# Reordering the start of an attention-and-experts kernel, with shared banks, other weight pieces and a scaling moved to ScalarE

## The chip, the cores and the metric

The kernel runs on one core of a Trainium2 chip. The metric is device time in microseconds (us) for one execution. One profiled execution of each kernel gives a trace; its span is about 2 us shorter than the time of the same execution. Engines are named as in the profile: PE is TensorE's matmuls, PEld its weight loads (they overlap PE), DVE is VectorE, ACT is ScalarE, POOL is GpSimd, SP is the engine that issues the transfers. PEclk is the clock granted to TensorE, with 1.00 as full speed.

A ratio is the mean time of one kernel's fast runs over that of the other's of the same rounds on the same chip, so it is not quite the ratio of the medians that stand beside it.

## The reference, cut to what matters

A linear attention with decay over 4 batches, 8 heads, 768 positions and 48 channels gives x of 3072 x 384. Then four experts, each 384 to 1024 to 384 with a relu, are summed with weights made from `domain_probs`.

```python
# attention, per position t
cur = einsum('bhd,bhe->bhde', u * kt, vt)
y[:, :, t] = einsum('bhd,bhde->bhe', rt, state + cur)
state = w * state + einsum('bhd,bhe->bhde', kt, vt)
# experts
p = domain_probs / (domain_probs.sum(-1, keepdims=True) + 1e-09)
for e in range(4):
    h = maximum(x @ w1[e], 0.0)
    out += p[:, e:e + 1] * (h @ w2[e])
```

## The kernel before

Attention goes in 24 chunks of 128 positions; four chunks, one of each batch, make a group. A chunk passes through these steps: RK (R and K scaled by powers of the decay, two products on DVE; the product `ruk` and the rounded `Vb` on POOL beside them), its transposes RKT, the products At, their mask AtM, Y and its sum Ysb, the state S, and the transpose xTe that feeds the experts.

The experts go in slots, one for each expert and group: layer 1 is 8 F blocks of 3 matmuls of 512 columns with a relu each, layer 2 is four times 8 matmuls of 384 columns. Attention steps of later chunks are woven in between. Every layer's product lands in one of four banks of PSUM with the tag "mm". The first group has no earlier work to hide behind, so its four chunks and expert 0 are written out by hand, with filler matmuls (`spin`) that keep the clock up.

Weights arrive as f32 in three pieces an array and are rounded to bf16 by ACT, DVE and POOL, one piece each.

```python
def load_w1(e):                       # 3 pieces, one for each 128 rows of the input dimension
    for db in range(NDB):
        t = staged[1, e, db] = work.tile([128, 3 * Dm], F32, tag="wst", bufs=8, name="wst")
        nc.sync.dma_start(t[:, 0:F], w1_v[e][:, db, :])
# ...
def wu_consts():
    nc.scalar.activation(w_row, w_row, AF.Ln)
    ps = psum.tile([128, 2, NP * C], F32, tag="At", bufs=1, name="wu_ps")
    spin(6)
    nc.tensor.matmul(ps[:, 0, 0:HD], ones, w_row, start=True, stop=True)
    nc.tensor.matmul(ps[:, 1, 0:HD], ones, u_row, start=True, stop=True)
# ...
def pre_a(ci):
    Rt, Kt, Vt = ins.pop(ci)
    RK = RKB[ci % NRK]
    nc.vector.tensor_mul(RK[:, 0, :, 0:D], Rt, W1_sd)
    nc.vector.tensor_mul(RK[:, 1, :, 0:D], Kt, W2_sd)
    # ...
    nc.gpsimd.tensor_mul(ruk, Rt, Kt)
    nc.gpsimd.tensor_mul(ruk, ruk, U_sd)
    nc.gpsimd.tensor_copy(Vb, Vt)
# ...
def l1(e, sc, fb, s0, n):             # one F block: a bank and a relu of its own
    # ... 3 matmuls into ps[:, 0:n, :]
    nc.scalar.activation(hTs[:, fb, s0:s0 + n, :], ps[:, 0:n, :], AF.Relu)
# ... in l2:
if e == 0:
    nc.vector.tensor_scalar(oaccs[ci], ps, scalar1=pe, scalar2=None, op0=ALU.mult)
# ... in the schedule, at (slot, place in the slot):
casts = {(0, 4): w2_on(1) + [lambda: (load_w2(2), load(6))],     # w2_on: pieces on A, V, P
         (0, 9): w1_on(2) + [lambda: (load_w1(3), load(7))],     # w1_on: pieces on P, A, V
         (1, 4): w2_on(2) + [lambda: load_w2(3)],
         (1, 8): w1_on(3), (2, 3): w2_on(3)}
```

## Time and profile before

| | before |
|---|---|
| median of 4 runs | 331.14 us (329.76 to 332.17) |
| profiled span | 329.9 us |
| PE, DVE, ACT, POOL busy | 93%, 56%, 45%, 34% |
| PE idle in the first 100 us | 17.6 us of the 23 us in the whole span |
| from the second group's first layer 1 (88.27) to the end | 241.6 us |

The holes of PE are in the first 90 us; the prediction shows the slices, the stretches and the milestones. What it did not show is what VectorE did in the hole just before the loop's second slot (58.86). This is the timeline of the kernel before: start and duration in us, engine, line, operation, output and input, shapes, count.

```profile
56.27 0.78 DVE L85 CAST w_sb<-wst 128x1024 bf16<-128x1024 f32 x1
...
57.36 0.55 DVE L210 TENSOR_TENSOR RK<-Rt,W_sd 128x384 bf16<-128x384 f32 x1
57.48 1.32 POOL L87 CAST w_sb<-wst 128x1024 bf16<-128x1024 f32 x1
57.82 1.39 DVE L211 TENSOR_TENSOR RK<-Kt,W_sd 128x384 bf16<-128x384 f32 x1
```

VectorE rounds a piece of 1024 columns in 0.78 us. POOL rounds its own from 57.48 to 58.80, and the matmul at 58.86 waits for that. In the same hole VectorE scales RK of chunk 5. The first half begins 0.12 us before POOL's rounding and takes 0.55 us; the second begins while POOL rounds, ends 0.41 us after POOL is done, and takes 1.39 us. PE stands anyway, so RK costs nothing here.

The rows of groups concerned (line, engine, operation, tiles, shapes, count; busy us, mean ns; idle time before and its releaser):

```profile
L344 DVE TENSOR_SCALAR oacc<-out_ps,p_nat 128x384 f32<-128x384 f32 x24 | 14.8, 617 | 23.7 <-PE out_ps L338 23.3
...
L211 DVE TENSOR_TENSOR RK<-Kt,W_sd 128x384 bf16<-128x384 f32 x24 | 20.9, 870 | 0.0
```

### The profile page before, as it was taken

Reading aid. Unit: us, or ns where it says so; the run is one execution under the profiler, and the core shown is the slowest. Engines: PE = TensorE matmul, PEld = TensorE weight load, DVE = VectorE, ACT = ScalarE, POOL = GpSimd, SP = SyncE. Lnnn points to the kernel's source line nnn. Section 1 sums busy time; section 2 is a strip of 40 time slices with the busy share of each in tenths; the row PEclk is TensorE's granted clock in tenths of the full one; section 3 lists DMA queues with packets and bytes.
Section 4 is the critical chain, followed back from the end, with each engine's and each line's share of the span. In section 5 each row is a group of like instructions: output and inputs, shape, how many; then the busy total and the mean of one; then the engine's idle time right before and its main releaser. Section 6 shows DMA issues by size and latency. Waiting matters only on the chain.

```text
span 329.9 us, 5731 instructions
## 1 busy us (share of the span) xinstructions
PE 306.9 (93%) x2251; PEld 174.0 (53%) x2286; DVE 184.6 (56%) x336; ACT 147.3 (45%) x260; POOL 111.3 (34%) x145
## 2 busy tenths in 40 slices
PE   7976776797999999999999999999999999999995
PEld 2444553454555555555555555555555555555552
DVE  3578536687657657657656666665644644222222
ACT  3432464555344454445435544544444543444440
POOL 2655602677424424433532541541703300000000
PEclk9999797999999999999999999999999999999999
DMA  7999999982154033054213144303020000110002
GB/s 209 287 221 363 286 263 230 223 241 50 32 119 119 6 69 73 0 145 97 42 32 72 33 121 88 59 16 74 25 74 0 2 0 2 48 47 2 0 2 96
DMA packets 84431, 31.89 MB, mean 97 GB/s; under 512 B 75674, under 2 KB 82844, under 8 KB 84404
## 3 DMA queue, kind: packets, MB, share of 16 engines
q1 hardware_dynamic: 84390, 31.52, 37.5%
q8 instruction: 18, 0.29, 0.4%
q14 instruction: 9, 0.07, 0.1%
q10 hardware_dynamic: 14, 0.00, 0.0%
HBM read 26.79 MB, written 4.72 MB: 96 GB/s over the span
## 4 chain that ended last, share of the span: by engine, by line
PE 86%; DVE 8%; issue 2%; ACT 2%; POOL 1%; POOLq 0%; ACTq 0%; DVEq 0%
PE out_ps L338 37%; PE hT_ps L325 36%; PE RKT_ps L234 3%; PE At_ps L249 2%; PE spin_ps L161 2%; DVE AtM L255 2%; PE Y_ps L273 1%; DVE RK L211 1%; PE St_ps L294 1%; PE xT_ps L312 1%; PE Y_ps L266 1%; ACT RKT L242 1%; DVE RK L210 1%; DVE Ysb L277 1%; DVE oacc L344 1%
## 5 line engine op out<-in xcount | busy, mean ns | idle before, releaser
L329 ACT ACTIVATE hTs<-hT_ps 128x512 bf16<-128x512 f32 (+2 forms) x220 | 114.6, 544 | 132.6 <-PE hT_ps L325 128.2
L325 PE MATMUL hT_ps<-xTe,w_sb 128*128 128x512 bf16 (+2 forms) x625 | 142.3, 355 | 4.4 <-POOL w_sb L87 1.9
L338 PE MATMUL out_ps<-w_sb,hTs 128*128 128x384 bf16 x768 | 140.0, 326 | 0.0
L338 PEld LDWEIGHTS <-hTs 128*128 128x128 bf16 x768 | 72.5, 98 | 51.7
L325 PEld LDWEIGHTS <-w_sb 128*128 128x128 bf16 x660 | 58.2, 99 | 49.6 <-POOL w_sb L87 2.4
L346 DVE SCALAR_TENSOR_TENSOR oacc<-out_ps,p_nat,oacc 128x384 f32<-128x384 f32 x72 | 44.5, 617 | 61.2 <-PE out_ps L338 59.6
L224 POOL TENSOR_TENSOR dv<-Vt,dcoef 128x384 f32<-128x384 f32 x24 | 19.9, 830 | 70.8 <-DVE dcoef L223 70.8
L255 DVE TENSOR_TENSOR AtM<-At_ps,mask 128x512 bf16<-128x512 f32 x48 | 30.9, 686 | 22.9 <-PE At_ps L249 22.9
L306 POOL TENSOR_TENSOR S<-Tn,wC 64x192 bf16<-64x192 f32 x32 | 16.4, 514 | 80.2 <-DVE Tn L305 79.0
L242 ACT COPY RKT<-RKT_ps 128x1024 bf16<-128x1024 bf16 x20 | 20.2, 1012 | 24.3 <-PE RKT_ps L234 24.3
L344 DVE TENSOR_SCALAR oacc<-out_ps,p_nat 128x384 f32<-128x384 f32 x24 | 14.8, 617 | 23.7 <-PE out_ps L338 23.3
L215 POOL TENSOR_TENSOR ruk<-ruk,U_sd 128x384 f32<-128x384 f32 x24 | 25.0, 1042 | 5.2 <-ACT U_sd L173 3.4
L214 POOL TENSOR_TENSOR ruk<-Rt,Kt 128x384 f32<-128x384 f32 x24 | 25.3, 1053 | 4.0 <-DMA Kt<-in_k_dram 2.9
L210 DVE TENSOR_TENSOR RK<-Rt,W_sd 128x384 bf16<-128x384 f32 x24 | 21.2, 882 | 4.4 <-ACT W_sd L171 4.3
L211 DVE TENSOR_TENSOR RK<-Kt,W_sd 128x384 bf16<-128x384 f32 x24 | 20.9, 870 | 0.0
L277 DVE TENSOR_TENSOR Ysb<-Y_ps,dv 128x384 bf16<-128x384 f32 x24 | 13.3, 556 | 10.0 <-PE Y_ps L273 8.6
L234 PE MATMUL RKT_ps<-ident,RK 128*128 128x128 bf16 x192 | 15.5, 220 | 2.7 <-DVE RK L210 1.5
L216 POOL CAST Vb<-Vt 128x384 bf16<-128x384 f32 x24 | 17.4, 724 | 0.0
L234 PEld LDWEIGHTS <-RK 128*128 128x128 bf16 x192 | 12.6, 99 | 7.1 <-DVE RK L210 2.3
L161 PE MATMUL spin_ps<-mask,ident 128*128 128x512 bf16 x41 | 14.1, 477 | 1.8 <-POOL mask masks.py:66 1.8
L223 DVE TENSOR_REDUCE dcoef<-ruk 128x8 f32<-128x384 f32 x24 | 13.0, 544 | 2.0 <-POOL ruk L215 2.0
L313 DVE COPY xTe<-xT_ps 128x384 bf16<-128x384 bf16 x24 | 8.6, 357 | 9.7 <-PE xT_ps L312 9.6
(53 smaller groups left out, 132.8 us busy)
## 6 DMA issues: line engine op xcount, KB each, us to landing
wst<-in_moe_w_dram SPq DMA_DIRECT2D x12, 512.0 KB, 5.2
Rt<-in_r_dram SPq DMA_DIRECT2D x24, 192.0 KB, 2.9
Kt<-in_k_dram SPq DMA_DIRECT2D x24, 192.0 KB, 3.1
Vt<-in_v_dram SPq DMA_DIRECT2D x24, 192.0 KB, 2.7
wst<-in_moe_w_dram SPq DMA_DIRECT2D x8, 576.0 KB, 5.9
out_dram<-oacc SPq DMA_DIRECT2D x24, 192.0 KB, 1.9
wst<-in_moe_w_dram SPq DMA_DIRECT2D x4, 384.0 KB, 6.5
prow<-in_moe_domain_probs_dram SPq DMA_DIRECT2D x1, 48.0 KB
```

What stands on the lines that cost most here:

```text
L161: nc.tensor.matmul(ps, ident, mask[:, None, :].to_broadcast((128, 4, 128)), start=True, stop=True)
L210: nc.vector.tensor_mul(RK[:, 0, :, 0:D], Rt, W1_sd)
L211: nc.vector.tensor_mul(RK[:, 1, :, 0:D], Kt, W2_sd)
L214: nc.gpsimd.tensor_mul(ruk, Rt, Kt)
L215: nc.gpsimd.tensor_mul(ruk, ruk, U_sd)
L234: nc.tensor.transpose(ps[:, i, q, :], s["RK"][:, i, 2 * q:2 * q + 2, :].rearrange("p a b -> p (a b)"), ident)
L242: nc.scalar.copy(s["RKT"], ps)
L255: nc.vector.tensor_mul(s["AtM"][:, j], ps[:, j], mask[:, None, :].to_broadcast((128, NP, C)))
L325: nc.tensor.matmul(ps[:, 0:n, :].rearrange("p a b -> p (a b)"), w1_sb[:, e, db, fb * 128:(fb + 1) * 128], xTe[:, db, s0:s0 + n, :].rearran ...
L329: nc.scalar.activation(hTs[:, fb, s0:s0 + n, :], ps[:, 0:n, :], AF.Relu)
L338: nc.tensor.matmul(ps, hTs[:, fb, s, :], w2_sb[:, e, fb, :], start=(fb == 0), stop=(fb == NFB - 1))
L346: nc.vector.scalar_tensor_tensor(oaccs[ci], in0=ps, scalar=pe, in1=oaccs[ci], op0=ALU.mult, op1=ALU.add)
```

## The change

Its intent is to take waits out of the first 90 us. It has five parts.

1. Preamble: the products for w and u get banks of their own, and 6 + 8 fillers become 2 + 1. The row of u comes over ACT's queue, and the inputs of chunk 2 are issued before expert 0's w2.
2. The first group's order is written anew for each engine: scaling of RK, POOL's part and the diagonal term are separate steps; RKT goes to ACT from chunk 1 on; expert 1 no longer starts before the loop.
3. In the first group four F blocks share a bank and one relu of 512 columns (`l1q`), 8 relus instead of 32.
4. w1 comes in F pieces (3, 3 and 2 blocks of 128 columns, three rows of 384 or 256 each), is rounded by ACT, DVE, ACT, one piece at a place of the slot; w2 keeps its pieces and is rounded the same way. All of expert 0's are rounded by ACT. POOL rounds none.
5. Expert 0's result is scaled by ACT instead of DVE.

```diff
+    PIECES = ((0, 3), (3, 6), (6, 8))
     def load_w1(e):
-        for db in range(NDB):
-            nc.sync.dma_start(t[:, 0:F], w1_v[e][:, db, :])
+        for i, (a, b) in enumerate(PIECES):
+            nc.sync.dma_start(t[:, 0:(b - a) * Dm].rearrange("p (d f) -> p d f", d=NDB),
+                              w1_v[e][:, :, a * 128:b * 128])
# ...
     def wu_consts():
-        ps = psum.tile([128, 2, NP * C], F32, tag="At", bufs=1, name="wu_ps")
-        spin(6)
+        wp = psum.tile([128, HD], F32, tag="ys", bufs=1, name="wu_ps")
+        up = psum.tile([128, HD], F32, tag="mm", bufs=4, name="wu_ps")
+        spin(2)
# ...
+    def l1q(e, sc, fb0, s):
+        ps = psum.tile([128, 4, 128], F32, tag="mm", bufs=4, name="hT_ps")
+        for i in range(4):
+            for db in range(NDB):
+                nc.tensor.matmul(ps[:, i, :], w1_sb[:, e, db, (fb0 + i) * 128:(fb0 + i + 1) * 128],
+                                 xTe[:, db, s, :], start=(i == 0 and db == 0),
+                                 stop=(i == 3 and db == NDB - 1), skip_group_check=True)
+        nc.scalar.activation(hTs[:, fb0:fb0 + 4, s, :], ps, AF.Relu)
# ... in l2
-            nc.vector.tensor_scalar(oaccs[ci], ps, scalar1=pe, scalar2=None, op0=ALU.mult)
+            nc.scalar.mul(oaccs[ci], ps, pe)
# ... the first group, its part around chunks 2 and 3 (the old order of these steps left out)
+        stY(2)
+        scale_rk(3)
+        ruk_vb(3)
+        spin(2)
+        stX(2)
+        stRK(3)
+        p_consts()
+        l1q(0, 0, 0, 2)
+        l1q(0, 0, 4, 2)
# ... the slots
-        casts = {(0, 4): w2_on(1) + [lambda: (load_w2(2), load(6))],
-                 (0, 9): w1_on(2) + [lambda: (load_w1(3), load(7))],
+        casts = {(0, 1): [lambda: cast_w2(1, 0, "A")], (0, 2): [lambda: cast_w2(1, 1, "V")],
+                 (0, 6): [lambda: cast_w2(1, 2, "A"), lambda: (load_w2(2), load(6))],
+                 (0, 7): [lambda: cast_w1(2, 0, "A")], (0, 8): [lambda: cast_w1(2, 1, "V")],
+                 (0, 10): [lambda: cast_w1(2, 2, "A"), lambda: (load_w1(3), load(7))],
# ... likewise for slots 1 and 2
```

## The prediction

> **What bounds the kernel now.** I read the page from the top: busy shares, the 40 slices, the chain that ended last, then the waits, the stretches and the timeline of the first 100 us. One core, span 329.9 us.
>
> ```profile
> PE   7976776797999999999999999999999999999995
> ...
> PEclk9999797999999999999999999999999999999999
> DMA  7999999982154033054213144303020000110002
> ...
> PE 86%; DVE 8%; issue 2%; ACT 2%; POOL 1%; POOLq 0%; ACTq 0%; DVEq 0%
> ```
>
> Each digit is the busy share of 8.2 us, in tenths. PE is full from the eleventh slice on; only the first ten have holes, and there the clock dips twice and the DMA engines are full for some 70 us. The chain of waits is 86% PE, and its non-PE parts lie early. The stretches put numbers on it (length; PE, PEld, DVE, ACT, POOL busy; clock; DMA share; GB/s):
>
> ```profile
> 0.00:16.00 16.00, 13.92 (x64) 5.93 (x65) 6.90 (x26) 6.05 (x10) 7.07 (x16) 1.00 0.88 243
> 16.00:45.00 29.00, 21.46 (x230) 15.11 (x228) 19.75 (x42) 10.76 (x35) 14.06 (x17) 0.94 1.00 279
> 45.00:60.00 15.00, 10.13 (x93) 6.15 (x94) 8.14 (x14) 7.45 (x20) 4.69 (x5) 0.89 0.97 264
> 60.00:76.00 16.00, 15.07 (x127) 8.49 (x127) 12.20 (x21) 9.77 (x15) 9.88 (x14) 1.00 0.87 206
> 76.00:100.00 24.00, 21.82 (x169) 12.26 (x171) 16.23 (x27) 10.53 (x17) 11.97 (x15) 1.00 0.32 74
> 100.00:330.00 230.00, 224.52 (x1579) 126.04 (x1606) 121.35 (x208) 102.71 (x167) 63.62 (x82) 1.00 0.20 47
> ```
>
> PE is idle 5.5 us in the last 230 us, of which some 3.8 us is the tail (last matmul ends at 326.05, then the last sum and the store). In the first 100 us it is idle 17.6 us, and part of its "busy" time there is filler: 41 spin matmuls, 14.1 us. The gain can only come from before the steady state. The timeline fixes the milestones (start, us, engine, line):
>
> ```profile
> 7.29 3.59 PE L161 MATMUL spin_ps<-mask,ident 128*128 128x512 bf16 x8
> ...
> 8.49 0.56 DVE L211 TENSOR_TENSOR RK<-Kt,W_sd 128x384 bf16<-128x384 f32 x1
> ...
> 10.68 0.72 PE L234 MATMUL RKT_ps<-ident,RK 128*128 128x128 bf16 x8
> ...
> 16.10 1.53 PE L325 MATMUL hT_ps<-xTe,w_sb 128*128 128x128 bf16 x24
> ...
> 46.52 1.46 PE L338 MATMUL out_ps<-w_sb,hTs 128*128 128x384 bf16 x8
> ...
> 58.86 0.82 PE L325 MATMUL hT_ps<-xTe,w_sb 128*128 128x512 bf16 x3 [1.93 <-POOL w_sb L87]
> ...
> 73.32 1.46 PE L325 MATMUL hT_ps<-xTe,w_sb 128*128 128x512 bf16 x6
> ...
> 88.27 1.46 PE L325 MATMUL hT_ps<-xTe,w_sb 128*128 128x512 bf16 x6
> ```
>
> These are: the spins that hold PE until 10.88 although RK was ready at 9.05; the first transposes; the first layer 1 (16.1); the start of the loop of slots (46.5); and the first layer 1 of expert 2 (58.9, held by POOL's rounding of its weights), of expert 3 (73.3) and of the second group of chunks (88.3). From there the program is the same but for which engine scales expert 0, so the prediction is how far left the 88.3 moves.
>
> **What the Trainium skill says.** "TensorE: Matmul & The Clock Gate", section "What's actually happening": PE runs at half rate until it has been busy for a window of about 3.4 us, and again after an idle window. The trace agrees: spins are 0.43 us apart until 10.7 us, 0.21 us apart at 11.2; after the 2.45 us wait for Ysb ending at 32.75 the next 24 layer-1 matmuls take 2.48 instead of 1.53 us. So filler may be removed only where real work takes its place. "ScalarE: Activation LUTs", section "What ACT_TABLE_LOAD costs": an ACTIVATE costs a fixed part plus 0.833 ns per element, and a per-partition pointer operand adds 93 ns. The trace agrees: relu of 128 columns 278 ns, of 512 columns 598 ns; the exponential with a pointer scale on 384 columns 582 ns. "SBUF — State Buffer", section "Who interferes with whom": a VectorE instruction with two SBUF inputs contends with GpSimd reads. The trace agrees: RK from Kt takes 0.55 us with POOL idle, 1.35 us beside a POOL product. "DMA: Bandwidth & Descriptors", section "Why small descriptors are slow (HBM only)", explains why 192-byte input rows are worse than weight rows; the trace shows 370 to 390 GB/s in slices of weights alone and 160 to 210 where inputs mix in.
>
> **Part by part.**
>
> Preamble. Before, six cold spins delay the w product to 4.44; with two it starts once the ones are set (that memset ends at 3.35) and ends near 5.1 (1.64 us long). W has its own bank now, so the exponential no longer waits for the u product: 5.2 instead of 7.40, -2.2 us. RK(0) is then ready at about 6.9, and one spin instead of eight lets the transposes start at 7.0, not 10.68: -3.7 us. The chain transposes, RKT, At, AtM, Y, Ysb, xT, xTe took 5.4 us before and is unchanged, so layer 1 could start at 12.5 to 13. Its weights: DMA moved 2.33 MB by 10 us, load 0 and w1 of expert 0 are 0.59 + 1.57 MB; three roundings on ACT (1.15, 1.15, 0.83, from 9.5) end at 12.6. Part: -3.5 us.
>
> Chunks 1 to 3. Before, 16.1 to 46.5, 30.4 us, and with 4 of 8 F blocks of expert 1 inside (4 x 3 x 0.215 = 2.6 us). Laying the new order by hand with the durations above (dcoef 0.54, dv 0.83, AtM 1.29, RKT on ACT 1.01, Ysb 0.55, RK 1.1): AtM(1) ends near 18.4, layer 1 of chunk 1 runs at 20.5, Y(2) at 22, RKT(3) at 25.5, layer 1 of chunk 2 at 26.7, Y(3) at 30.4, and the loop starts near 35.6: 22.7 us. Four relus of 128 columns become one of 512: eight back to back took 1.48 to 2.24 us, two will take 1.1; 32 relus become 8. RKT no longer passes from DVE to ACT (ACT waited 9.8 us for that). Part: -7.7 us, of which 2.6 come back in the first slot.
>
> First slot, before 46.5 to 58.9 = 12.4 us. Work now: 8 blocks x 0.645 + one layer-2 group 1.30 + seven attention steps at 1.6 us a chunk (a steady slot takes 12.0 us, its two layers 10.4, and holds one chunk) = 8.4 us, plus 1.8 us of waits: 10.2. The POOL wait of 1.9 us goes, POOL rounds nothing. Part: -2.2 us, the returned 2.6 included.
>
> Next two slots: 14.4 and 15.0 us against 10.4 + 1.44 x 1.6 = 12.7 us of work. DVE no longer stands before expert 0's scaling (4.2 us of its wait at 48.0, in the slot before), and POOL's roundings no longer slow RK. Estimate 13.8 each: -1.8 us.
>
> Steady part. 20 scalings move from DVE (617 ns) to ACT (about 580): per such slot ACT has 8 x 0.60 + 1.0 + 4 x 0.58 = 8.1 of 12 us. Nothing there is bound by either: 0.
>
> Sum: -3.5 - 7.7 - 2.2 - 1.8 = -15.2 us. A schedule laid by hand has the shortest possible waits: the same sum on the old order would miss semaphore latencies and the two cold stretches (together 2 to 3 us). I also expect the DMA to take something. I take off 4 us for both: -11.2, so 319.5.
>
> **Rivals.** (1) DMA takes the place of the waits. Weights of all experts (12.6 MB) and the ten chunks loaded by then move at about 4.1 us an array and 3.5 us a chunk (18.6 MB by 70 us). In the new order w1 of expert 3 lands near 58.4 and w2 of expert 3 near 69.5; my schedule wants them at 56 to 60 and 68. That is even, so a slip of a few us is hidden or shown by luck. ACT now holds most of the roundings in its strict order, so a late weight also holds the relus. For it: DMA share 0.9 to 1.1 up to 70 us. Against it: SP was partly gated by buffers (3.6 us on ACT's, 2.2 on POOL's rounding), which come free earlier. If it bites fully, w2(3) at 72 puts the 88.3 at 79 to 82: 322 to 325. (2) The clock: 24 spins instead of 41; if PE idles over 2 to 3 us at chunk 1 or 2 and runs cold for 6 us, +2 to 3 us: 322. (3) ACT becomes the bound in the first slots by two of three roundings (2.0 of 3 us) beside relus, RKT and scalings: by count 8 x 0.6 + 1.4 x 1.0 + 4 x 1.05 = 10.4 us of a 13.8 us slot, close enough to hold PE now and then: +1 to 2 us. (4) Everything fits and nothing slips: 315.
>
> **Range and chances.** The rivals that add do not all add; the gains of the preamble and of chunks 1 to 3 are the surest, 6 us at least even with DMA late. Range 314 to 325. A 2% gain needs less than 324.2: 0.84; within 2%: 0.15; slower: 0.01.
>
> **What would show it.** Right: first transposes near 7, first layer 1 near 13, loop start at 36 to 39, the first layer 1 of the second group at 74 to 79, and 241 to 242 us from there to the end, as before; no PE wait for POOL. Wrong: PE or ACT waiting for the landing of expert 3's weights, matmuls at double length around 15 to 30 us, DVE standing at RK(2) for its inputs, or slots after 90 us longer than 12.0 us, which would mean that the scaling on ACT reaches PE through the four shared banks.

## The result, and the profile after

| | before | after |
|---|---|---|
| median of 4 runs | 331.14 us | 322.33 us (321.71 to 323.56) |
| ratio | | 0.9741, 95% interval 0.9692 to 0.9791 |
| profiled span | 329.9 us | 319.9 us (its execution took 321.71, the fastest of the four) |
| PE, DVE, ACT, POOL busy | 93%, 56%, 45%, 34% | 95%, 54%, 52%, 33% |

The change is 8.8 us faster by the medians. The 40 slices of the kernel after (each digit the busy share of 8.0 us in tenths; the clock and the DMA share likewise):

```profile
PE   6787887999999999999999999999999999999995
...
PEclk9997999999999999999999999999999999999999
DMA  7989998998541321540321540321110000200002
```

PE is full from the eighth slice on (the eleventh before). One dip of the clock is left, in the fourth slice, where there were two. The DMA engines are still full through the ninth slice, some 72 us, and then come and go with the groups. The chain that ended last, by engine:

```profile
PE 85%; DVE 10%; DMA 2%; ACT 1%; issue 1%; POOL 0%; SPq 0%; DVEq 0%; ACTq 0%
```

DVE has 10% of it, instead of 8%, and transfers appear with 2%. POOL is gone from it.

The stretches of the kernel after (from and to in us; length; busy us and count of PE, PEld, DVE, ACT, POOL; clock; DMA share; GB/s):

```profile
0.00:16.00 16.00, 11.75 (x75) 5.70 (x76) 9.91 (x29) 7.93 (x13) 7.34 (x16) 1.00 0.89 215
16.00:45.00 29.00, 23.46 (x253) 15.77 (x250) 19.60 (x37) 18.49 (x27) 12.08 (x13) 0.94 0.99 276
45.00:60.00 15.00, 12.26 (x99) 6.47 (x97) 11.56 (x20) 9.91 (x15) 7.55 (x10) 1.00 0.99 251
60.00:76.00 16.00, 14.78 (x125) 8.28 (x124) 12.64 (x21) 9.92 (x14) 6.71 (x9) 1.00 1.03 260
76.00:100.00 24.00, 24.00 (x187) 13.71 (x186) 13.79 (x25) 12.50 (x21) 9.61 (x12) 1.00 0.44 102
100.00:330.00 230.00, 216.26 (x1531) 120.48 (x1528) 106.19 (x181) 108.15 (x178) 60.96 (x78) 1.00 0.18 44
```

PE's idle time from 16 to 45 us falls from 7.5 us to 5.5 us, and from 45 to 60 us from 4.9 to 2.7 us. ACT carries 18.5 us of the 29 us, instead of 10.8. The clock in 16 to 45 us is 0.94 in both. If it is either full or half, as the Trainium skill has it in "TensorE: Matmul & The Clock Gate", section "What's actually happening", 0.94 over 29 us is (1 - 0.94) / 0.5 x 29 = 3.5 us at half rate: one of the windows of about 3.4 us that the page names. The kernel before had another of them in 45 to 60 us: 0.11 / 0.5 x 15 = 3.3 us. The runs agree with the page here, and the same sum is used below. The record of the clock in the packed traces has the windows themselves, 3.41 us each: from 27.1 to 30.5 us after; from 34.8 and from 51.9 us before. It begins only at some 10 us, so the 1.00 of the first stretch says nothing about the time before: fillers of 512 columns start 0.42 us apart at 8 us, and 0.21 us apart at 10.2 us.

The milestones of the kernel after, from its timeline:

```profile
6.72 1.06 PE L241 MATMUL RKT_ps<-ident,RK 128*128 128x128 bf16 x8
...
13.07 0.83 PE L346 MATMUL hT_ps<-xTe,w_sb 128*128 128x128 bf16 x12
...
37.95 1.46 PE L332 MATMUL hT_ps<-xTe,w_sb 128*128 128x512 bf16 x6
...
47.36 1.46 PE L332 MATMUL hT_ps<-xTe,w_sb 128*128 128x512 bf16 x6
...
64.82 1.46 PE L332 MATMUL hT_ps<-xTe,w_sb 128*128 128x512 bf16 x6
...
78.49 1.46 PE L332 MATMUL hT_ps<-xTe,w_sb 128*128 128x512 bf16 x6
```

They are the first transposes, the first layer 1, the loop's first slot, the end of expert 1's layer 1 with the first three matmuls of expert 2's (the record at 47.36 holds six, three of each, so expert 2 starts at 48.0), expert 3's first layer 1 and the second group's. Against the prediction's hand plan:

| stretch | before | planned | after | after minus planned |
|---|---|---|---|---|
| to the first layer 1 | 16.1 | 12.6 | 13.1 | +0.5 |
| chunks 1 to 3, to the loop | 30.4 | 22.7 | 24.9 | +2.2 |
| slot of expert 1 | 12.4 | 10.2 | 10.1 | -0.1 |
| slot of expert 2 | 14.5 | 13.8 | 16.8 | +3.0 |
| slot of expert 3 | 15.0 | 13.8 | 13.7 | -0.1 |
| from there to the end | 241.6 | 241.6 | 241.4 | -0.2 |

(In the kernel before, chunks 1 to 3 hold 2.6 us of expert 1's work, which the change gives back to the first slot.) The sum of the last column is 5.3 us, where the prediction had set aside 4 us for slips without saying at which stretch. So the total came out close, but one slot went the wrong way: expert 2's slot became 2.3 us longer than before.

What held it stands in VectorE's order around chunk 5, in the timeline of the kernel after (the bracket is the idle time before the instruction and what ended it):

```profile
46.25 1.34 DVE L86 CAST w_sb<-wst 128x1152 bf16<-128x1152 f32 x1
47.51 0.72 DVE L312 TENSOR_TENSOR Tn<-S,St_ps 64x192 f32<-64x192 bf16 x2
...
48.26 0.36 DVE L320 COPY xTe<-xT_ps 128x384 bf16<-128x384 bf16 x1
...
48.65 0.83 DVE L214 TENSOR_TENSOR RK<-Rt,W_sd 128x384 bf16<-128x384 f32 x1
...
49.14 1.19 POOL L222 TENSOR_TENSOR ruk<-Rt,Kt 128x384 f32<-128x384 f32 x1
49.40 1.35 DVE L215 TENSOR_TENSOR RK<-Kt,W_sd 128x384 bf16<-128x384 f32 x1
...
49.53 0.40 PE L241 MATMUL RKT_ps<-ident,RK 128*128 128x128 bf16 x4 [0.71 <-DVE RK L214]
...
50.80 0.40 PE L241 MATMUL RKT_ps<-ident,RK 128*128 128x128 bf16 x4 [0.87 <-DVE RK L215]
```

VectorE rounds its piece of expert 2's w1 (1.34 us), then does the state's sum, xTe of chunk 4, and only then RK of chunk 5. The second half of RK takes 1.35 us: it begins while POOL makes its product `ruk` (49.14 to 50.33), and ends 0.42 us after it. PE stands 0.71 us for the first half of RK and 0.87 us for the second, then 0.51 us for RKT from ACT. Before, this chain lay in the hole that POOL's rounding left open, as shown above. The hole is gone and the chain is in the open, one slot later.

The sum of that slot: PE is busy 14.1 of its 16.8 us and waits 2.5 us. The plan had 12.7 us of work and 1.1 us of waits. So half of the miss is waits. The other half is work counted too low: I took an average of 1.44 chunks for each slot, but the steps that fall in this slot hold the transposes, At and Y of two chunks. The kernel before could have told me: its same slot was busy 13.5 of 14.5 us.

One more thing is new in this order, a rounding of 1.34 us. The same engine rounds the same 1152 columns of w2 in 0.75 us, with POOL at rest in the first case:

```profile
54.82 0.75 DVE L86 CAST w_sb<-wst 128x1152 bf16<-128x1152 f32 x1
```

What differs is the shape. A piece of w1 now goes to three rows of 384 in the weights' tile, a piece of w2 to one run of 1152. The Trainium skill, "VectorE: DVE Perf Modes", section "Mode 2×_2P — use both read ports for one tensor", says that a copy of f32 in SBUF handles two elements a cycle where the outermost dimension is even (or odd and equal on both sides); the page's "Specifications" give the clock as 0.96 GHz. By an estimate from these, one element a cycle makes 1152 / 0.96 = 1.20 us, two make 0.60 us; with a fixed part of 0.15 us, fitted to the trace, these are the two durations. They fit the reading that the new pieces of w1 lost the faster mode: 0.59 us more for each such rounding than one run of the same length takes. No run here gives them an even number of rows, so the cause is read from the page and the two durations, not tested.

The rows of groups after, which answer to those of before:

```profile
L365 ACT ACTIVATE oacc<-out_ps,p_nat 128x384 f32<-128x384 f32 x24 | 14.0, 583 | 19.3 <-PE out_ps L359 18.4
L215 DVE TENSOR_TENSOR RK<-Kt,W_sd 128x384 bf16<-128x384 f32 x24 | 23.9, 997 | 0.0
```

Expert 0's scaling on ACT takes 583 ns, as estimated, against 617 ns on DVE. RK from Kt did not get faster: its mean went from 870 to 997 ns.

### The profile page after: what moved, and what is told of

It reads as the page before. It is cut to its first block, busy times and chain, and to the rows that moved or that the text cites. A ratio compares the mean times of both kernels' runs of the same rounds, so it can differ in the third digit from the quotient of the medians.

```text
span 319.9 us, 5705 instructions
## 1 busy us (share of the span) xinstructions
PE 302.5 (95%) x2257; PEld 170.4 (53%) x2257; DVE 173.7 (54%) x308; ACT 166.9 (52%) x265; POOL 104.3 (33%) x137
## 4 chain that ended last, share of the span: by engine, by line
PE 85%; DVE 10%; DMA 2%; ACT 1%; issue 1%; POOL 0%; SPq 0%; DVEq 0%; ACTq 0%
PE out_ps L359 38%; PE hT_ps L332 34%; PE RKT_ps L241 3%; DVE AtM L262 3%; PE At_ps L256 2%; DMA wst<-in_moe_w_dram 2%; DVE RK L215 2%; PE Y_ps L280 2%; PE hT_ps L346 1%; DVE RK L214 1%; PE xT_ps L319 1%; ACT RKT L249 1%; PE Y_ps L273 1%; PE St_ps L301 1%; DVE Ysb L284 1%
## 5 line engine op out<-in xcount | busy, mean ns | idle before, releaser
L336 ACT ACTIVATE hTs<-hT_ps 128x512 bf16<-128x512 f32 x184 | 107.9, 599 | 91.2 <-PE hT_ps L332 88.5
L332 PE MATMUL hT_ps<-xTe,w_sb 128*128 128x512 bf16 x552 | 137.7, 379 | 0.0
L332 PEld LDWEIGHTS <-w_sb 128*128 128x128 bf16 x552 | 50.7, 98 | 45.7
L313 POOL TENSOR_TENSOR S<-Tn,wC 64x192 bf16<-64x192 f32 x32 | 16.1, 502 | 85.5 <-DVE Tn L312 78.6
L249 ACT COPY RKT<-RKT_ps 128x1024 bf16<-128x1024 bf16 x23 | 23.2, 1011 | 22.0 <-PE RKT_ps L241 22.0
L222 POOL TENSOR_TENSOR ruk<-Rt,Kt 128x384 f32<-128x384 f32 x24 | 24.9, 1037 | 12.1 <-DMA Kt<-in_k_dram 10.9
L223 POOL TENSOR_TENSOR ruk<-ruk,U_sd 128x384 f32<-128x384 f32 x24 | 26.1, 1087 | 3.1 <-ACT U_sd L177 1.3
L365 ACT ACTIVATE oacc<-out_ps,p_nat 128x384 f32<-128x384 f32 x24 | 14.0, 583 | 19.3 <-PE out_ps L359 18.4
L215 DVE TENSOR_TENSOR RK<-Kt,W_sd 128x384 bf16<-128x384 f32 x24 | 23.9, 997 | 0.0
L214 DVE TENSOR_TENSOR RK<-Rt,W_sd 128x384 bf16<-128x384 f32 x24 | 22.3, 931 | 2.2 <-ACT W_sd L175 2.1
L284 DVE TENSOR_TENSOR Ysb<-Y_ps,dv 128x384 bf16<-128x384 f32 x24 | 13.4, 557 | 13.7 <-PE Y_ps L280 11.9
L84 ACT CAST w_sb<-wst 128x1152 bf16<-128x1152 f32 (+1 forms) x18 | 17.9, 1010 | 0.2 <-DMA wst<-in_moe_w_dram 0.2
L312 DVE TENSOR_TENSOR Tn<-S,St_ps 64x192 f32<-64x192 bf16 x32 | 11.2, 349 | 6.4 <-PE St_ps L301 5.9
```

The costliest lines, as they stand in the source:

```text
L222: nc.gpsimd.tensor_mul(ruk, s["Rt"], s["Kt"])
L249: nc.scalar.copy(s["RKT"], ps)
L332: nc.tensor.matmul(ps[:, 0:n, :].rearrange("p a b -> p (a b)"), w1_sb[:, e, db, fb * 128:(fb + 1) * 128], xTe[:, db, s0:s0 + n, :].rearran ...
```

## The experiments

The second group's first relu is the milestone used for all of them: in every run, from there to the end of the span are 240.5 to 240.7 us, so it carries the result of a profile. For the kernel before it stands at 89.2 us, after at 79.4 us; the first relus of the slots of expert 1, 2 and 3 after are at 38.9, 49.1 and 65.7 us. "Slot of expert 2" is the distance of the last two: 16.6 us.

### One part undone at a time

The four kernels ran on one chip in 3 rounds; the kernel before had 331.86 us there.

**e1: the preamble as it was.** One bank for both products, fillers 6 and 8.

```diff
-        wp = psum.tile([128, HD], F32, tag="ys", bufs=1, name="wu_ps")
-        up = psum.tile([128, HD], F32, tag="mm", bufs=4, name="wu_ps")
-        spin(2)
+        ps = psum.tile([128, 2, NP * C], F32, tag="At", bufs=1, name="wu_ps")
+        wp, up = ps[:, 0, 0:HD], ps[:, 1, 0:HD]
+        spin(6)
# ...
-        spin(1)
+        spin(8)
```

> Undoes one part: six spins before the w product, eight before the first transposes, and w and u in one bank again. Theory PE chain (what was won early reaches the end): first transposes back at 10 to 10.7 us, start of the second group's layer 1 about 3.5 us later than 78.5, time near 325.5 to 326. Rival DMA (the DMA engines are full up to 72 us and set when the expert weights come, so an earlier start is hidden): second group within 1.5 us of 78.5, time near 322.5 to 323.5.

Measured: 323.12 us, ratio 0.9749 (0.9708 to 0.9791); span 322.1. The first transposes are back at 10.68 us, 4.0 us later; the second group's first relu is at 81.6 us, only 2.2 us later. Almost half of what the preamble gives is lost again at once: the first group's second relu is 2.2 us later already (19.0 against 16.8 us).

**e2: expert 0 scaled on DVE again.**

```diff
-            nc.scalar.mul(oaccs[ci], ps, pe)
+            nc.vector.tensor_scalar(oaccs[ci], ps, scalar1=pe, scalar2=None, op0=ALU.mult)
```

> Undoes one part: expert 0 is scaled on VectorE again. Theory: it matters only in the first group and the slot after it, where VectorE stands before a scaling while layer 2 isn't done; 4 scalings of 0.6 us there, so 0.5 to 2 us longer (323 to 324.5), steady slots 12.0 us in both. Rival (it was ScalarE's added work that made the second slot 16.8 us): that slot becomes shorter and the time is 1 us or more below 322.3.

Measured: 322.76 us, ratio 0.9731 (0.9708 to 0.9755); span 320.8, milestone 80.3 us. It moves the start by 0.9 us in this profile and nothing in the steady part. But 0.7 us of this is there at the first relu of chunk 2 (30.1 against 29.4 us), before the first scaling (34.3 us), and this profile has one half-rate window more. So the profile leaves the scaling 0.2 us at most.

**e3: the third piece of each array but the first rounded by POOL.** The order stays, and w1 of expert 0 stays on ACT.

```diff
-            cast_w2(0, i, "A")
+            cast_w2(0, i, "AAP"[i])
# ...
-            cast_w1(1, i, "AVA"[i])
+            cast_w1(1, i, "AVP"[i])
# ... and "A" to "P" for the third piece of w2(1), w1(2), w2(2), w1(3), w2(3)
```

> Undoes one part: the third piece of each weight group but the very first is rounded on GpSimd as before (pieces on ScalarE, VectorE, GpSimd). Theory of the prediction (GpSimd's roundings delayed PE by a late cast and slowed RK): RK's mean in the first 80 us rises, PE waits once or twice on a GpSimd cast, 1 to 3 us longer, 323.5 to 325.5. Rival (GpSimd's ruk products alone already slow RK, the roundings add nothing): within 1 us of 322.3.

Measured: 322.81 us, ratio 0.9740 (0.9705 to 0.9774); span 322.4, milestone 81.9 us, the slot of expert 2 at 18.5 us, which here holds a half-rate window (53.3 to 56.7 us). RK in this run:

```profile
L214 DVE TENSOR_TENSOR RK<-Rt,W_sd 128x384 bf16<-128x384 f32 x24 | 22.8, 950 | 2.2 <-ACT W_sd L175 2.1
L215 DVE TENSOR_TENSOR RK<-Kt,W_sd 128x384 bf16<-128x384 f32 x24 | 22.9, 955 | 0.0
```

In the changed kernel the two means are 931 and 997 ns, and 925 and 962 ns when it ran again (e5). So POOL's roundings add nothing to RK that shows, as the expectation's rival said.

**e4: a bank and a relu for each F block again.**

```diff
         hTs, xTe = hTss[e, sc], get_xTe(sc)
-        ps = psum.tile([128, 4, 128], F32, tag="mm", bufs=4, name="hT_ps")
         for i in range(4):
-            for db in range(NDB):
-                nc.tensor.matmul(ps[:, i, :], ...)
-        nc.scalar.activation(hTs[:, fb0:fb0 + 4, s, :], ps, AF.Relu)
+            l1(e, sc, fb0 + i, s, 1)
```

> Undoes one part: each F block of a chunk in the first group has its own bank and its own relu of 128 columns again, 32 relus instead of 8. Theory: relus are 32 x 0.278 = 8.9 us against 8 x 0.6 = 4.8 us of ScalarE, some of it on the path to the first layer 2 and before RKT copies and roundings in ScalarE's order: 1 to 2.5 us longer, 323.5 to 325. Rival (ScalarE has room there): within 0.7 us of 322.3.

Measured: 323.22 us, ratio 0.9742 (0.9715 to 0.9768); span 323.4, milestone 82.8 us. The stretch of its profile from 16 to 45 us:

```profile
16.00:45.00 29.00, 23.16 (x222) 15.47 (x221) 17.34 (x35) 17.26 (x43) 11.07 (x13) 0.82 0.95 274
```

A clock of 0.82 is 0.18 / 0.5 x 29 = 10.4 us at half rate, three windows instead of one.

What follows from the four. By their profiles they cost 2.2, 0.9, 2.5 and 3.4 us, 9.0 us together, which looks like the whole gain of 9.8 us told apart. It is not. The profiled execution of e3 took 324.30 us and that of e4 325.14 us, each the slowest of its kernel's runs, both with a mean clock of 0.984; the other runs of the same kernels, with 0.989 to 0.995, took 322.27 to 323.33 and 322.68 to 323.23 us. The profile of the changed kernel was the fastest of its runs. By the medians, and against the changed kernel run again on the same chip (e5, 322.19 us), the parts cost 0.9, 0.6, 0.6 and 1.0 us, with intervals of 0.8 to 1.4 us to either side. So each part taken away alone costs about one us or less, and the four added make 3.1 of the 9.7 us gained on this chip. What is left lies in the order itself or in what the parts do together. The order (part 2) was not undone alone: the other parts are written into it.

### What holds the slot of expert 2

The second set asked which of three things holds that slot. Three kernels take one each away, e5 is the changed kernel again, 5 rounds on the same chip, before 331.93 us.

**e5: the changed kernel again.**

> The changed kernel itself, unedited, for the spread on the chip that the others of this call run on. Both theories: 322 to 323, ratio 0.972 to 0.976; milestones in its profile within 1.5 us of 38.9 (first relu of the loop), 49.1, 65.7 and 79.4 (first relus of the next three slots).

Measured: 322.19 us (321.71 to 322.57), ratio 0.9715 (0.9694 to 0.9735); span 320.1, milestone 79.5 us, slot of expert 2 16.2 us.

**e6: POOL's product one chunk early.** `ruk` and `Vb` of the next chunk are made with Y of this one, so RK runs beside no product of POOL.

```diff
-                yield lambda ci=ci: stY(ci)
+                yield lambda ci=ci: (stY(ci), ci + 1 < last and ruk_vb(ci + 1))
# ... ruk_vb returns at once if the chunk was done; inputs are read without being popped
```

> One thing moved: GpSimd's products ruk and Vb of a chunk are issued one chunk ahead, after Y of the chunk before, so that they no longer run beside VectorE's RK products. Theory V (the second slot is 16.6 us because VectorE's order holds RK(5): two RK of 0.8 and 1.35 us behind a rounding of 1.34): RK back to about 0.56 us each in the first 80 us, second slot 14 to 15.5 us, time 1 to 2.5 us below the unedited run beside it. Rival D (DMA landings set the slot): RK faster, slot unchanged at 16 to 17, time within 0.5 us.

Measured: 321.70 us, ratio 0.9704 (0.9676 to 0.9732); span 320.1. RK from Kt fell to a mean of 644 ns over the whole run, so the contention is real and mostly gone (in the first 80 us the mean is 797 ns, against 1082 in e5). But the slot of expert 2 takes 17.1 us, and the milestone stays at 79.5 us. The group of RK, and the waits of this kernel from 45 to 68 us (engine, line; releaser; us in total, times, longest):

```profile
L215 DVE TENSOR_TENSOR RK<-Kt,W_sd 128x384 bf16<-128x384 f32 x24 | 15.5, 644 | 0.2 <-DMA Kt<-in_k_dram 0.2
```

```profile
POOL ruk L225 <- DMA Kt<-in_k_dram: 12.4, 3, 5.6
...
DVE w_sb L86 <- DMA wst<-in_moe_w_dram: 1.3, 2, 1.0
```

POOL now asks for the inputs a chunk earlier and waits 12.4 us for Kt; VectorE's roundings wait 1.3 us for weights (0.4 us in the changed kernel). By these waits the transfers, full in this stretch, are the next hold; e6 with e8's edit alone was not run.

**e7: all rounding on ACT.** VectorE rounds nothing.

```diff
-            cast_w1(1, i, "AVA"[i])
+            cast_w1(1, i, "AAA"[i])
# ... and "V" to "A" for the second piece of w2(1), w1(2), w2(2), w1(3), w2(3)
```

> One thing changed: the middle pieces of the weights of experts 1 to 3 are rounded on ScalarE too, so VectorE rounds nothing. Theory V: VectorE loses six roundings of 0.75 to 1.35 us in the first 75 us and RK(5), xTe and AtM come earlier, second slot 14.5 to 16, time 0.5 to 2 us below the unedited run. Rival A (ScalarE is the next bound: 10.4 of 13.8 us by count, now 2 roundings more a slot): relus late, slots longer, time 0.5 to 2 us above it.

Measured: 323.15 us, ratio 0.9742 (0.9713 to 0.9771); span 321.4, milestone 80.8 us. The slot of expert 2 falls to 15.4 us and that of expert 3 to 13.0 us, so VectorE's rounding did hold them. But the loop starts 1.4 us later than in e5 (0.4 us of it stands at chunk 2's relus, before any rounding differs, in a profile with one half-rate window more) and the slot of expert 1 grows to 11.6 us, where PE waits 2.6 us for RKT from ACT instead of 1.2 us: ACT, by the prediction's third rival near its limit there, becomes the hold.

**e8: inputs of later chunks issued later**, so that weights come first.

```diff
-        if ci >= SUB and loaded[0] < TOTC:
+        if ci >= SUB + 2 and loaded[0] < TOTC:
```

> One thing moved: each chunk's inputs from the ninth on are loaded two chunks later, so 1.2 MB of inputs no longer stand in the DMA queue before the weights of experts 2 and 3. Rival D: w1 and w2 of expert 3 are issued 4 to 7 us earlier than 55.0 and 65.7, second slot 1 us or more shorter, time 1 to 3 us below the unedited run. Theory V: earlier landings but no wait of PE or VectorE hung on them except 0.4 us, time within 0.7 us of the unedited run.

Measured: 321.86 us, ratio 0.9706 (0.9680 to 0.9731); span 320.1. Expert 3's w1 is issued at 51.3 instead of 55.0 us and its w2 at 60.1 instead of 65.7 us, and no milestone differs from e5's by 0.1 us. So the landing of weights alone does not hold the change as it is: rival 1 is out for this kernel.

### The order of VectorE, and everything together

The third set, 5 rounds on another chip, before 330.89 us.

**e9: VectorE's w1 rounding behind RK of the next chunk.**

```diff
-                 (0, 7): [...], (0, 8): [lambda: cast_w1(2, 1, "V")],
+                 (0, 7): [...],
# ...
+                 (1, 0): [lambda: cast_w1(2, 1, "V")],
# ... likewise cast_w1(3, 1, "V") from (1, 10) to (2, 0)
```

> One thing moved: VectorE's two roundings of first-layer weights (experts 2 and 3) are issued later in its order, that of expert 2 behind RK(5), that of expert 3 behind Y(6). Theory V (VectorE's order in front of RK(5) holds PE at the start of the second slot): RK(5) begins near 47.4 instead of 48.65, PE's wait of 1.6 us for it shrinks by about 1.2, the second slot's first relu to the third's falls from 16.3 to 16.6 us to about 15 to 15.5, time 0.5 to 1.5 us below 322.2. Rival (the slot has other holds of the same size right behind it): slot still 16 or more, time within 0.5 us.

Measured: 321.52 us, ratio 0.9708 (0.9680 to 0.9736); span 319.7. RK of chunk 5 starts at 48.39 us, though everything else in this run, which has one half-rate window more, is 0.4 us later than in the changed kernel's profile; the slot of expert 2 takes 15.5 us.

```profile
48.39 0.78 DVE L214 TENSOR_TENSOR RK<-Rt,W_sd 128x384 bf16<-128x384 f32 x1
49.09 1.34 DVE L215 TENSOR_TENSOR RK<-Kt,W_sd 128x384 bf16<-128x384 f32 x1
50.36 1.34 DVE L86 CAST w_sb<-wst 128x1152 bf16<-128x1152 f32 x1
```

The slot of expert 3 takes 0.5 us more than in the changed kernel, so the milestone, 79.2 us, moves by 0.2 to 0.4 us only.

**e10: xTe of chunk 2 before RK of chunk 3.** In the changed kernel PE waits 1.7 us for this xTe: chunk 3's transposes need the bank that it still holds.

```profile
26.70 0.69 PE L241 MATMUL RKT_ps<-ident,RK 128*128 128x128 bf16 x8 [1.66 <-DVE xTe L320]
```

```diff
         stY(2)
-        scale_rk(3)
-        ruk_vb(3)
         spin(2)
         stX(2)
-        stRK(3)
-        p_consts()
+        scale_rk(3)
+        ruk_vb(3)
         l1q(0, 0, 0, 2)
         l1q(0, 0, 4, 2)
+        stRK(3)
+        p_consts()
```

> One thing moved, in the first group: xTe of the third chunk is copied before RK of the fourth, and its layer 1 runs before the transposes of the fourth. Theory: PE's wait of 1.7 us for xTe and its cold stretch (24 matmuls in 2.73 instead of 1.5 us) go, loop starts 1.5 to 2.5 us earlier than 38.9 to 39.4, time 0.5 to 2 us below 322.2. Rival (the fourth chunk's chain, put back behind the third's layer 1, takes it again): loop start within 0.7 us of before, time within 0.5 us.

Measured: 321.28 us, ratio 0.9701 (0.9673 to 0.9730); span 319.0. That wait is gone. The loop starts 1.0 us earlier than after (first relu at 37.8 us; 1.6 us earlier than in e5), and 0.9 us of it is left at the second group (78.5 us).

**e11: together.** e6, e8, e9 and e10, and the inputs of chunk 5 issued before expert 2's w1.

```diff
-        load_w1(2)
         load(5)
+        load_w1(2)
# ... and the edits of e6, e8, e9 and e10
```

> For a faster version: e6's early products, e8's later inputs, e9's later roundings and e10's order together, and inputs of chunk 5 issued before the first-layer weights of expert 2. Theory V: loop start 37 to 38, second group's first relu 75.5 to 77.5 instead of 79.5, time 318.5 to 320.5, ratio 0.960 to 0.966. Rival (DMA and VectorE are so near to each other that each gives way to the other): second group 78.5 or later, time 321 to 322.

Measured: 317.65 us (317.36 to 318.77), ratio 0.9596 (0.9568 to 0.9624). This beats both kernels. Its slices:

```profile
PE   6796988989999999999999999999999999999995
...
PEclk9999999999999999999999999999999999999999
DMA  7999998990583000683000674000550000200002
```

The clock has no dip left in its record. The loop starts at 37.2 us, the second group's first relu is at 75.3 us, and the slot of expert 2 takes 14.4 us. The place shown above for the changed kernel, here:

```profile
46.31 0.78 DVE L214 TENSOR_TENSOR RK<-Rt,W_sd 128x384 bf16<-128x384 f32 x1
...
47.02 0.55 DVE L215 TENSOR_TENSOR RK<-Kt,W_sd 128x384 bf16<-128x384 f32 x1
...
47.16 0.86 PE L244 MATMUL RKT_ps<-ident,RK 128*128 128x128 bf16 x8
47.49 1.34 DVE L86 CAST w_sb<-wst 128x1152 bf16<-128x1152 f32 x1
```

RK of chunk 5 starts 2.3 us earlier than after (1.6 us of it because the loop starts earlier), its second half takes 0.55 us, all eight transposes run in one go, without a wait named, and the rounding comes behind them.

**e12: the same with POOL's product where the change had it.**

```diff
# against e11
-                yield lambda ci=ci: (stY(ci), ci + 1 < last and ruk_vb(ci + 1))
+                yield lambda ci=ci: stY(ci)
```

> As the run before it, but with GpSimd's products where the change has them. Theory V: RK stays at 0.8 and 1.35 us, 0.5 to 1.5 us slower than the run before it. Rival (early products wait for the inputs' landing and gain nothing, as their 12.4 us wait for Kt in e6 hints): equal to it or up to 0.7 us faster.

Measured: 319.23 us (318.79 to 319.68), ratio 0.9636 (0.9609 to 0.9662). RK of chunk 5 from Kt is back at 1.35 us, and the milestone at 77.4 us. So the early product is worth 1.6 us by medians in this order (1.3 us by means; the slowest of e11's five runs is still below the fastest of e12's, by 0.02 us, while the intervals of the ratios, which share the noise of the kernel before, do overlap), and was worth nothing that can be told from zero alone: e6 minus e5 is -0.5 us by medians, with no move in the profile.

What follows from the set: removed alone, the holds give 0.5 us (e6) and 0.3 us (e8) against e5 on the same chip by medians, which the runs do not tell from zero. For e9 and e10 the chip was another, so their ratios are the measure: 0.9708 and 0.9701 against 0.9715 of e5, with intervals of 0.003 either way. Together, with the swap of chunk 5's inputs, they give, by the ratios, 0.9715 - 0.9596 = 0.0119, or 3.9 us of 331, and 4.1 us at the milestone. A part of this can be the clock: the mean clock is 0.994 to 1.000 in e11's runs and 0.989 to 0.995 in e5's, and a window of 3.4 us at half rate can cost PE up to 1.7 us. How much, no run tells. The reading that fits all of them, not shown for each step of it, is that the holds lie next to one another: behind VectorE's order stands the contention with POOL, and behind that the order of transfers, as e6's waits show.

## Why the prediction was right or wrong

The time, 322.33 us, lies in the range of 314 to 325, and it is faster by more than 2%, to which the prediction gave 0.84. The point was 2.8 us too low by the median; by the spans the gain was 10.0 us where 11.2 was forecast, in the fastest execution of the four. By its own steps:

- **What bounds the kernel, and where the gain can come from: right.** From the second group's first layer 1 to the end, 241.6 us became 241.4 us. "Nothing there is bound by either: 0" held, with ACT's scaling at 583 ns.
- **Preamble, -3.5 us: right in size,** -3.0 us measured at the first layer 1. What e1 adds is that only 2.2 us of 4.0 reach the second group in its profile, and 0.9 us the time.
- **Chunks 1 to 3, -7.7 us: right in mechanism, 2.2 us too short.** 24.9 us, not 22.7. The hand plan had no wait of 1.7 us for xTe(2) at the shared transpose bank, no 0.9 us of Y for the state, and the layer 1 behind it was cold, 2.73 us where 1.50 us is the warm duration. e10 confirmed the first of these; the loop started 1.0 to 1.6 us earlier without it.
- **First slot, -2.2 us: right.** 10.1 us against 10.2 us, and no wait of PE for POOL's rounding is left in the profile.
- **"Next two slots ... DVE no longer stands before expert 0's scaling ..., and POOL's roundings no longer slow RK. Estimate 13.8 each": this is the step that failed.** Expert 3's slot took 13.7 us, expert 2's 16.8 us: where 1.8 us were to be gained, 1.1 us were lost. POOL's roundings did go, and one of them had indeed stood beside RK of chunk 5. But POOL's product `ruk` slows RK alike, and took its place: RK from Kt went from 870 to 997 ns on average, e3 put the roundings back and RK got no slower, and e6 brought it to 644 ns by moving POOL's part of a chunk alone. The prediction quotes 1.35 us "beside a POOL product" in its own second part and then counts on the roundings only. It also did not ask what the hole that it closed had hidden: RK of chunk 5. The rest of the miss is work, 14.1 us where 12.7 us was counted.
- **The 4 us taken off: near in size, for partly wrong reasons, so in part by luck.** The slips were 5.3 us, 3.0 of them in the slot that failed. It was meant for latencies, the clock and the DMA. Latencies and one cold window came (about 2 us in chunks 1 to 3). The DMA cost PE nothing that e8 could take away.
- **Rival 1, the DMA: wrong for this kernel, right one step on.** Its share stayed near 1 up to 72 us, and no matmul waited for a weight; VectorE's rounding waited 0.4 us once, which is how transfers come to 2% of the chain. e8 brought weights 4 to 6 us earlier and moved nothing. But in e6, where another hold was gone, its waits suggest that it took over.
- **Rival 2, the clock: came in part.** One window is left, as before in the same stretch, and with it came a sign that the prediction had named for being wrong, matmuls at double length: the 24 of chunk 2's layer 1, from 27.9 us. The profiles of e3 and e4 show three windows.
- **Rival 3, ACT: not the hold in the change, but close,** as e7 shows, where some 1.0 us more at the loop's start and 1.3 us in the slot of expert 1 come from moving VectorE's roundings to it.

What stays open: the timed worth of each part of the change and of the new order by itself; the swap of chunk 5's inputs and expert 2's w1, which ran only inside e11; and whether a shape of w1's pieces that keeps the faster rounding would give back its 0.59 us a rounding, and what PE would gain from that.

## What to carry to other kernels

Before you count a removed wait as gained, list what else runs in that hole on every engine: the chain that it hid comes into the open next, often one stage later, as RK of chunk 5 did here. Where several holds lie next to one another, removing one alone shows nothing, and that does not clear it: e6 alone gave nothing that could be told from zero, and 1.6 us with the others gone. And one profiled execution can be the slow one of its kernel, so set its time beside the other runs' before sizing a part from it.

## What the Trainium skill lacked or had wrong

- "SBUF — State Buffer", section "Who interferes with whom", says that a VectorE instruction with two SBUF inputs contends with reads of GpSimd. The runs agree, and give a size that the page lacks for it: RK of 128 x 384 in f32 takes 0.55 us alone, and 1.35 us where it begins shortly after POOL's product (it ends 0.42 us after that); where it began 0.12 us before POOL's instruction, it took 0.55 us. Moving the products took its mean from 997 to 644 ns.
- "VectorE: DVE Perf Modes", section "Mode 2×_2P — use both read ports for one tensor", gives the condition as the outermost dimension even, or odd and equal on both sides. A piece written in three rows of 384 has three rows in the program's views of both sides, so by that wording it might have kept the mode; it took 1.34 us, against 0.75 us for the same 1152 columns in one run. Whether the source, which lies in one run, counts as three rows or as one, the page's section does not say, and no run here tells.
- "TensorE: Matmul & The Clock Gate": nothing wrong was seen. The dips of the granted clock come to 3.5, 3.3 and 10.4 us at half rate, about one, one and three of the windows that the page names.
- "DMA: Bandwidth & Descriptors", section "Why small descriptors are slow (HBM only)": the page's overheads do not give a rate for such a mix. With w1 in rows of 1536 bytes or less instead of 4096, and inputs in rows of 192, the core moved 276 GB/s from 16 to 45 us, against 279 before. That is no test of the row length, since inputs make 1.7 MB of that stretch after and 2.4 MB before. Packet by packet in the traces, from 2 to 75 us, one of 4096 bytes took 188 ns on average before, one of 1536 bytes 77 ns after, and one of 192 bytes 16 ns in both: 21.8, 20.1 and 12.1 bytes a ns.
